# First steps of a staged Fourier transform, on quarters with sums and differences, in a fused GFNet mixing and SoLU kernel

## The chip, the cores and the metric

The kernel runs on one core of a Trainium2 chip. The metric is the device time of one execution in microseconds (us). Before the change four runs took 1708.62 to 1714.92 us, with a median of 1712.42 us.

## What is computed

The first half filters each of eight sequences of 3136 tokens with 256 channels in the frequency domain. The second half takes all 25088 filtered tokens through a two-layer block with a SoLU activation and a layer norm. Everything is float32 at the outputs.

```python
# x (8, 3136, 256), filt_r and filt_i (1569, 256)
X = np.fft.rfft(x, axis=1)
y = np.fft.irfft(X * (filt_r + 1j * filt_i), n=3136, axis=1)
t = y.reshape(8 * 3136, 256)
h = t @ w_in                                   # w_in (256, 1024)
e = np.exp(h - h.max(-1, keepdims=True))
solu = h * e / (e.sum(-1, keepdims=True) + 1e-9)
ln = (solu - solu.mean(-1, keepdims=True)) / np.sqrt(solu.var(-1, keepdims=True) + 1e-6) * g_ln
out = ln @ w_out                               # w_out (1024, 256)
```

## The kernel before

**The transform.** A length of 3136 is 49 times 64. Token number n1*64+n2 has n1 from 0 to 48 and n2 from 0 to 63. For each sequence ("entry", 0 to 7) three stages follow each other:

- *First steps* (`first`, L204; matmuls at L211, named pa). The 64 values of n2 are taken in 8 pieces. A piece has four values from the front and their four mirrored ones (63-n2) from the back. `fetch_x` (L194) loads it as a tile of 98 rows, 49 for each of the two halves, by 4x256. Two matmuls ("halves" u=0 and u=1) multiply it with the constant table wf (98x100), each over 512 columns (two values of n2 times 256 channels). Table rows of the mirrored half carry signs, so that sums and differences over the mirrored pair are taken inside the matmul. ScalarE (ACT) copies each result out of PSUM into a tile t1 (L213), and `store_first` (L215, L217) stores it to a scratch d1 in DRAM.
- *Spectrum* (`forward` L242, `multiply` L251, `inverse` L267). In 7 units, the second step on 64x64 blocks (matmuls at L239, named pb), the product with the filter (VectorE, L260 to L262; the last addition or subtraction of some units is on GpSimd), and the first step of the way back (again L239, named pc). The pb and pc matmuls have 64 rows and 64 columns of weights each and lie in the four quadrants of the array. The result is stored in a scratch d2.
- *Steps back* (`fetch_back` L285, `back` L294; matmuls at L300, named py). In 8 pieces of two groups each they write the filtered tokens, channels on partitions, into the resident tile y.

Entry 0 runs through all this ahead of the main loop. Entries 1 to 7 run inside it.

**The main loop.** `step(k)` (L837) is called for k from 0 to 204. A step handles one block of 128 tokens, and two steps, an even and an odd one, make a pair, in which both matrix products are done with seven instead of eight block products (sums of blocks come from GpSimd: `pair_sums` L607 and `project_sums` L713, both through L605). m (L627) are the matmuls of the first product, o (L739) those of the second. Between them: ACT keeps a half of h (L637), VectorE finishes h with its extremum (L648, L651), ACT takes the exponential (L659), VectorE normalizes (L675), ACT squares (L677), VectorE turns the block in 32x32 squares (L685), SyncE's queue regroups it by DMA to solu_t (L697), and the outputs are scaled (L751 to L758) and stored.

**The order of the work.** Nothing is scheduled by a tool: the instructions are issued in the order in which `step` calls them, and each engine goes through its own in that order. Per step there are lists of jobs: `stores[k]` at the start, `products[k]` in the middle of VectorE's work, `early[k]` and `mid[k]` between the matmuls, `late[k]` at the end, then `loads[k]`. The table PLAN gives, for each of entries 1 to 7, the steps of its 8 first pieces, 7 spectrum units and 8 pieces back. The half u=0 of a first piece stands in `early[t]`, u=1 in `late[t]`.

**Buffers and queues.** x tiles and the tiles t4 of the way back share a pool "r" of three buffers, t1 has a pool of three. Row loads are put into `loads` by a rule:

```python
row_loads.sort(key=lambda load: load[0])
for n, (t, earliest, load) in enumerate(row_loads):
    at = max(t - 3, earliest, min(row_loads[n - 3][0] + 1, t - 1) if n >= 3 else -1)
```

so a load stands at the end of step `at`, at most three steps ahead of its use t and not before the row tile three uses earlier is done. The x loads, the d1 and d2 stores, the t4 loads and the filter loads are issued on GpSimd's queue (POOL), between its sums. PSUM results pa, py and one of the m tiles take turns in two banks (`psum`, L515).

Of the kernel before, what the change touches and what calls it, by code (L numbers as in the profile page):

```python
# [17 lines left out]
P = 128  # L18
# [20 lines left out]
    ([0, 0, 0, 0, 1, 1, 1, 1], [4, 5, 6, 7, 8, 10, 12], [16, 17, 18, 19, 20, 20, 21, 22]),  # L39
    (range(3, 11), range(14, 28, 2), range(31, 47, 2)),  # L40
    ([11, 12, 13, 14, 15, 24, 26, 28], range(32, 46, 2), range(53, 69, 2)),
    (range(32, 48, 2), range(50, 64, 2), range(76, 92, 2)),
    (range(54, 70, 2), range(72, 86, 2), range(101, 117, 2)),
    (range(77, 93, 2), range(95, 109, 2), range(125, 141, 2)),
    (range(102, 118, 2), range(120, 134, 2), range(150, 166, 2)),
]
EPS_LN, EPS_SM = 1e-6, 1e-9


def dft_tables():  # L50


# [31 lines left out]
    f32 = np.float32  # L84
    return wf.reshape(NR, NK).astype(f32), wi.reshape(NK, NR).astype(f32), de.astype(f32)


@with_exitstack
def kernel(
# [9 lines left out]
):  # L99
    nc = tc.nc  # L100
    wf_host, wi_host, de_host = dft_tables()
    wf_dram = nc.inline_tensor(wf_host, name="wf_tbl").ap()
    wi_dram = nc.inline_tensor(wi_host, name="wi_tbl").ap()
    de_dram = nc.inline_tensor(de_host, name="de_tbl").ap()
# [13 lines left out]

    wf_t = consts.tile([NR, NK], FP32, name="wf_t")
    wi_t = consts.tile([NK, NR], FP32, name="wi_t")  # L120

# [47 lines left out]
    class Spectrum:  # L169
# [5 lines left out]
        def __init__(self, e, pools, load, load_de):  # L175
            self.e, self.pools = e, pools
            self.load, self.load_de = load, load_de
            self.spare = {}
            self.units = [(i, min(2, NP - i)) for i in range(0, NP, 2)]
            self.xs, self.t1s, self.t2s, self.fs, self.prods, self.gs, self.des, self.spectra = (  # L180
                {} for _ in range(8))

# [32 lines left out]
        def store_first(self, i, n0, store):  # L215
            t1 = self.t1s.pop((i, n0))
            store(d1[self.e].rearrange("s (a n) c -> (s a) n c", a=4)[  # L217
                :, NCH * i + n0:NCH * i + n0 + t1.shape[1], :], t1)

        def buffer(self, i, kind, shape):  # L220
# [86 lines left out]
    with ExitStack() as st:  # L307
# [158 lines left out]
        for i in range(units):  # L466
            if i + 2 < units:
                start(i + 2)
            sp.multiply(i, 0, nc.vector.tensor_tensor)
            sp.multiply(i, 1, nc.gpsimd.tensor_tensor)  # L470
            pss = [ps_t.tile([P, 2, C], FP32, name=f"pc_0_{i}_{u}", tag="t") for u in range(2)]
            idle(pss[0])
            sp.inverse(i, pss)
            sp.store(i, nc.scalar.dma_start)
            if i == 0:
                nc.gpsimd.dma_start(out=wi_t, in_=wi_dram)
                nc.gpsimd.dma_start(out=g_sb, in_=moe_g_ln.rearrange("(k p) -> p k", p=P))
            elif i in (1, 3, 4):
                begin({1: 2, 3: 3, 4: 4}[i])
# [38 lines left out]
    def psum_pair(name, other):  # L518
# [11 lines left out]
    pools |= {name: pool(name + "1", bufs)  # L530
             for name, bufs in (("r", 3), ("t1", 3), ("t2", 1), ("p", 1), ("g", 1))}
    pools["de"] = pool("de1", 2)
# [228 lines left out]
    def store_out(p):  # L761
# [10 lines left out]


    early, mid, late, stores, loads, products = (
        [[] for _ in range(blocks + LAG + 1)] for _ in range(6))
# [9 lines left out]
    for e in range(1, B):  # L785
# [5 lines left out]
        for i, t in enumerate(first_at):  # L791
            if i not in sp.xs:
                row_loads.append((t, -1, lambda sp=sp, i=i: sp.fetch_x(
                    i, [lambda out, in_: nc.gpsimd.dma_start(out=out, in_=in_)] * 2)))
            for u in range(2):
                (early, late)[u][t].append(lambda sp=sp, i=i, u=u: sp.first(
                    i, (u,), psum(f"pa_{sp.e}_{i}_{u}").rearrange("p a c -> p (a c)").rearrange(
                        "p (o n) -> p o n", o=1), nc.scalar.copy))
                ((early[t], late[t]) if t < 2 else (mid[t], stores[t + 1]))[u].append(
                    lambda sp=sp, i=i, u=u: sp.store_first(i, 2 * u, nc.gpsimd.dma_start))  # L800
        for i, t in enumerate(spectrum_at):
# [17 lines left out]
        for ch, t in enumerate(back_at):  # L819
            row_loads.append((t, spectrum_at[-1] + 2, lambda e=e, ch=ch: fetch_back(e, ch, pools["r"])))  # L820
            for cb in range(KD):
                (early, late)[cb][t].append(
                    lambda e=e, ch=ch, cb=cb: back(e, ch, cb, nc.scalar.copy))
    row_loads.sort(key=lambda load: load[0])
    for n, (t, earliest, load) in enumerate(row_loads):


        at = max(t - 3, earliest, min(row_loads[n - 3][0] + 1, t - 1) if n >= 3 else -1)
        assert at < t
# [7 lines left out]
    def step(k):  # L837
# [39 lines left out]
        if not odd:  # L877
# [6 lines left out]
            if 0 <= j - 3 < pairs:  # L884
                regroup(j - 3, 1)
            for job in mid[k]:
                job()
            if 0 <= j - 4 < pairs:
# [3 lines left out]
        else:  # L892
# [5 lines left out]
            if hid:  # L898
                product(j, 3)
                product(j, 4)  # L900
            for job in mid[k]:
                job()
            if 0 <= j - 3 < pairs:
# [13 lines left out]
        else:  # L917
# [3 lines left out]
            if proj:  # L921
                keep_out(p, 1, (1, 0))
        for job in late[k] + loads[k]:
            job()
# [37 lines left out]
```

## Time and profile before

| | us |
|---|---|
| median of four runs | 1712.42 |
| the profiled execution | 1714.54 |
| its span, first to last instruction | 1712.8 |
| PE (TensorE matmul) busy | 1634.7 |
| VectorE (DVE) busy | 1215.5 |
| GpSimd (POOL) busy | 1102.6 |
| ScalarE (ACT) busy | 945.5 |
| matmuls pa, from x (L211), 232 records | 127.5 |
| matmuls py (L300), 1024 records | 138.0 |
| ACT copies t<-pa (L213), 112 | 65.4 |
| DMA issues x<-in_x_dram on POOL (L794), 100, 683 ns each | 67.9 |
| DMA issues d<-t on POOL (L217), 112, 574 ns each | 64.3 |

A float32 matmul leaves two records on PE. Matmul records overlap, so that the distance between starts tells what one costs. Times inside the execution are counted from the span's start. The main loop begins at about 111 us; a step takes some 7 to 9 us, a pair of steps some 14 us where no transform work is in it and 18.2 us (817 to 853) where first steps, spectrum and steps back fall together. "A <- B" in a wait reads: A stood idle until B was done. The profile's mean TensorE clock is 0.976 of full speed; DMA moved 308.72 MB.

### The profile page before, as it was taken

How to read it: one execution, taken by the hardware profiler on the slowest of the kernel's cores; microseconds unless marked ns; L12 is line 12 of the kernel's file. 1: busy time of each engine (PE TensorE's matmuls, PEld its weight loads, DVE VectorE, ACT ScalarE, POOL GpSimd, SP SyncE). 2: the span in 40 equal slices, each digit the busy share in tenths (PEclk: the TensorE clock that was granted, in tenths of full speed). 3: DMA queues.
4: the chain of work that ended last, by engine and by line, in shares of the span. 5: the costliest groups of instructions: out<-in, count | busy, mean ns of one | idle time of the engine just before them, and what ended most of it. 6: DMA issues, size and time to landing. Idle time of an engine off the chain costs nothing.

```text
span 1712.8 us, 30324 instructions
## 1 busy us (share of the span) xinstructions
PE 1634.7 (95%) x9816; PEld 1122.1 (66%) x9816; DVE 1215.5 (71%) x2583; ACT 945.5 (55%) x1734; POOL 1102.6 (64%) x1319
## 2 busy tenths in 40 slices
PE   6778899899999999999999999999999999999996
PEld 2353366666666666766677666766777777777776
DVE  1675676577776787677766787678877777777772
ACT  2144556465656556656566455655556666656551
POOL 5354876455766767757666667666756766667663
PEclk8978899899999999999999999999999999999999
DMA  9885878667886787667865786657754454444443
GB/s 258 242 265 172 269 239 228 178 169 181 236 248 178 193 238 216 169 162 216 240 180 143 198 233 181 159 146 219 214 131 111 112 140 114 102 111 106 109 108 93
DMA packets 367329, 308.72 MB, mean 180 GB/s; under 512 B 63802, under 2 KB 333011, under 8 KB 367171
## 3 DMA queue, kind: packets, MB, share of 16 engines
q1 hardware_dynamic: 287684, 147.59, 33.9%
q0 software_dynamic: 42592, 120.91, 23.8%
q10 hardware_dynamic: 36896, 38.28, 7.7%
q8 instruction: 80, 1.31, 0.3%
q14 instruction: 77, 0.63, 0.1%
HBM read 121.82 MB, written 81.50 MB: 119 GB/s over the span
## 4 chain that ended last, share of the span: by engine, by line
PE 74%; DMA 10%; DVE 8%; POOL 3%; issue 2%; ACT 2%; SPq 1%; POOLq 0%; ACTq 0%; DVEq 0%
PE o L739 29%; PE m L627 29%; PE py L300 6%; PE pa L211 5%; DMA solu_t<-turn 4%; PE pb L239 3%; DVE h L675 2%; PE pc L239 2%; DMA x<-in_x_dram 1%; DMA t<-d 1%; SPq L697 1%; DMA out_dram<-ot 1%; POOL u L605 1%; ACT e L659 1%; DMA t<-x 1%
## 5 line engine op out<-in xcount | busy, mean ns | idle before, releaser
L677 ACT ACTIVATE e<-h,nmu 128x1024 f32<-128x1024 f32 x196 | 225.4, 1150 | 332.3 <-DVE h L675 328.9
L739 PE MATMUL o<-w_out_sb,solu_t 128*128 128x128 f32 x3136 | 402.7, 277 | 2.8 <-DVE ot L756 1.9
L739 PEld LDWEIGHTS o<-w_out_sb,solu_t 128*128 128x128 f32 x3136 | 380.7, 193 | 33.8 <-issue 28.6
L739 PEld LDWEIGHTS o<-w_out_sb,u 128*128 128x128 f32 x2352 | 306.5, 192 | 146.0 <-issue 113.9
L627 PE MATMUL m<-w_in_sb,s 128*128 128x512 f32 x784 | 399.1, 600 | 1.1 <-ACT h L637 1.1
L605 POOL TENSOR_TENSOR u<-solu_t 128x512 f32<-128x512 f32 x98 | 149.3, 1524 | 271.2 <-DMA solu_t<-turn 142.1
L739 PE MATMUL o<-w_out_sb,u 128*128 128x128 f32 x2352 | 311.9, 276 | 7.3 <-ACT ot L751 6.6
L627 PE MATMUL m<-w_in_sb,y 128*128 128x512 f32 x588 | 310.5, 612 | 6.3 <-DVE nmax L651 4.0
L675 DVE SCALAR_TENSOR_TENSOR h<-e,rsum,h 128x1024 f32<-128x1024 f32 x196 | 279.4, 1425 | 6.9
L758 DVE SCALAR_TENSOR_TENSOR ot<-o,rs_t,ot 128x128 f32<-128x128 f32 x294 | 102.7, 349 | 249.7 <-ACT ot L751 206.5
L685 DVE STREAM_TRANSPOSE turn<-h 128x1024 f32<-128x1024 f32 x196 | 242.7, 1238 | 1.7 <-DMA rows<-rs 0.4
L637 ACT COPY h<-m 128x512 f32<-128x512 f32 x294 | 172.5, 587 | 125.3 <-PE m L627 122.2
L659 ACT ACTIVATE e<-h,nmax 128x1024 f32<-128x1024 f32 x196 | 224.9, 1148 | 0.0
L651 DVE CUSTOM_DVE_ANT_0 h<-m,h 128x512 f32<-128x512 f32 x196 | 134.4, 686 | 113.2 <-ACT h L637 84.0
L605 POOL TENSOR_TENSOR u<-solu_t,u 128x512 f32<-128x512 f32 x98 | 138.2, 1410 | 100.6 <-PE o L739 96.7
L627 PEld LDWEIGHTS m<-w_in_sb,s 128*128 128x128 f32 x784 | 131.2, 192 | 86.5 <-issue 78.6
L300 PEld LDWEIGHTS py<-wi_t,t 100*128 100x128 f32 x1024 | 135.9, 200 | 51.2 <-issue 41.9
L627 PEld LDWEIGHTS m<-w_in_sb,y 128*128 128x128 f32 x588 | 100.0, 195 | 81.6 <-issue 51.9
L605 POOL TENSOR_TENSOR solu_t<-solu_t,solu_t 128x512 f32<-128x512 f32 x98 | 146.5, 1495 | 7.7
L300 PE MATMUL py<-wi_t,t 100*128 100x98 f32 x1024 | 138.0, 282 | 13.1 <-DMA t<-d 8.9
L303 ACT COPY y<-py 128x392 f32<-128x392 f32 x128 | 108.1, 846 | 69.8 <-PE py L300 67.0
L211 PE MATMUL pa<-x,wf_t 98*100 98x512 f32 x232 | 127.5, 643 | 11.9 <-DMA x<-in_x_dram 10.1
(96 smaller groups left out, 1931.9 us busy)
## 6 DMA issues: line engine op xcount, KB each, us to landing
solu_t<-turn SPq DMA_DIRECT2D x784, 128.0 KB
out_dram<-ot SPq DMA_DIRECT2D x196, 128.0 KB
d<-t POOLq DMA_DIRECT2D x112, 200.0 KB, 4.7
t<-d POOLq DMA_DIRECT2D x56, 400.0 KB, 5.3
x<-in_x_dram POOLq DMA_DIRECT2D x108, 196.0 KB, 5.7
f<-f_dram POOLq DMA_DIRECT2D x39, 512.0 KB, 7.1
d<-g POOLq DMA_DIRECT2D x39, 512.0 KB, 6.1
t<-d ACTq DMA_DIRECT2D x36, 512.0 KB
```

Of the source, the lines that this page charges most:

```text
L211: nc.tensor.matmul(out=ps[0:NK, j], lhsT=wf_t, rhs=self.xs[i][0:NR, 2 * u:2 * u + 2, :], start=True, stop=True)
L300: nc.tensor.matmul(out=psv[:, i:2 * NCH - i:2 * NCH - 1 - 2 * i, :], lhsT=t4s[e, ch][:, i, cb * P:cb * P + P], rhs=wi_t, start=True, stop= ...
L303: evac(out=y[:, cb, t0:t0 + S].rearrange("p (r m j) -> p m j r", m=N2 // NCH, j=NCH)[:, ch:last + 1 - ch:last - 2 * ch], in_=psv.rearrange ...
L605: nc.gpsimd.tensor_tensor(out=out, in0=in0, in1=in1, op=op)
L627: nc.tensor.matmul(out=ms[j, bank], lhsT=lhsT, rhs=w_in_sb[:, w, :], start=m in (1, 2, 7), stop=True, skip_group_check=True)
L637: nc.scalar.copy(out=h_half(k, i), in_=ms[j, 0])
L651: nc.vector.tensor_tensor_reduce(out=h_half(k, i), in0=ms[j, bank], in1=h_half(*kept), scale=1.0, scalar=sofar, op0=ALU.add, op1=ALU.min, ...
L659: nc.scalar.activation(out=e, in_=hs[k], func=AFT.Exp, bias=nmaxs.pop(k)[:, 1:2], scale=-1.0, accum_out=esum)
L675: nc.vector.scalar_tensor_tensor(out=solu, in0=e, scalar=rsum, in1=solu, op0=ALU.mult, op1=ALU.mult, accum_out=nmu)
L677: nc.scalar.activation(out=e, in_=solu, func=AFT.Square, bias=nmu, scale=-float(DFF), accum_out=variances[g][:, i:i + 1])
L685: nc.vector.transpose(out=turns[g][:, :, i, :], in_=solus.pop(k).rearrange("p (f j) -> p f j", j=32))
L739: nc.tensor.matmul(out=pos[p, bank], lhsT=lhs[:, f, :], rhs=w[:, f, :], start=f == 0 and m in (1, 2, 7), stop=True, skip_group_check=True)
```

## The change

It touches the first steps of entries 1 to 7, the table PLAN and the rule for row loads.

- Entries 2 to 7: a piece is loaded by `fetch_quarters` with its rows 0 to 48 holding two of the four values n2 and rows 64 to 112 the other two, and with the mirrored values in the columns beside them, so that sum and difference over the mirrored pair can be taken elementwise. Four loads take the place of two; for the first group 64 rows are read instead of 49, save in entry 7. `difference` (VectorE) writes a new tile, for which there is one buffer; `sum` (GpSimd) is done in place.
- `first_quarters` multiplies with a new table wq (128x2x64): four matmuls over 512 columns, 49 rows each, with 64 columns of weights for the sums and 50 for the differences, one in each quadrant of the array. ACT makes two copies of 114 rows by 512 back into the x tile, and `store_quarters` stores it with two DMAs of 50 rows by 4 KB.
- In a piece's step t, which is odd: the loads stand at the end of step t-3, or up to t-2 where a buffer is not free sooner; the difference stands in `products[t-1]` and the sum at the end of step t-1, ahead of that step's loads; the matmuls stand at the end of step t (or in the early place for the first of two pieces with the same t); the stores stand at the start of step t+1.
- Entry 1 keeps its matmuls, but copies results back into its x tile and stores right after each.
- Pool "r" has four buffers instead of three and the rule looks four uses back; pool t1 is gone. wq is loaded once on GpSimd's queue before the main loop.
- Steps back stand in even steps, spectrum units start in even steps too.

```diff
 PLAN = [
     None,
     ([0, 0, 0, 0, 1, 1, 1, 1], [4, 5, 6, 7, 8, 10, 12], [16, 17, 18, 19, 20, 20, 21, 22]),
-    (range(3, 11), range(14, 28, 2), range(31, 47, 2)),
-    ([11, 12, 13, 14, 15, 24, 26, 28], range(32, 46, 2), range(53, 69, 2)),
-    (range(32, 48, 2), range(50, 64, 2), range(76, 92, 2)),
-    (range(54, 70, 2), range(72, 86, 2), range(101, 117, 2)),
-    (range(77, 93, 2), range(95, 109, 2), range(125, 141, 2)),
-    (range(102, 118, 2), range(120, 134, 2), range(150, 166, 2)),
+    ([3, 5, 7, 9, 9, 11, 11, 13], range(16, 30, 2), range(32, 48, 2)),
+    ([15, 23, 25, 27, 29, 31, 33, 35], range(38, 52, 2), range(54, 70, 2)),
+    (range(39, 55, 2), range(58, 72, 2), range(76, 92, 2)),
+    (range(63, 79, 2), range(82, 96, 2), range(100, 116, 2)),
+    (range(87, 103, 2), range(106, 120, 2), range(126, 142, 2)),
+    (range(111, 127, 2), range(130, 144, 2), range(150, 166, 2)),
 ]
...
+        def fetch_quarters(self, i, dma):
+            self.xs[i] = out = self.pools["r"].tile([P, NCH, C], FP32, name=f"x_{self.e}_{i}", tag="r")
+            xb = x[self.e]
+            for g in range(2):
+                for h, first, step in ((0, NCH * i + 2 * g, C), (1, N2 - 1 - NCH * i - 2 * g, -C)):
+                    parts = [(64, N1)] if g else [(0, 64)] if self.e + 1 < B else [(0, N1), (N1, 64 - N1)]
+                    for p, n in parts:
+                        dma(out=out[p:p + n, 2 * h:2 * h + 2, :],
+                            in_=bass.AP(tensor=xb.tensor, offset=xb.offset + first * C,
+                                        ap=[[N2 * C, n], [step, 2], [1, C]]))
+        def difference(self, i):
+            rows = slice(0, 64 + N1)
+            xi = self.xs[i]
+            self.diffs[i] = diff = self.pools["diff"].tile([P, 2, C], FP32, name=f"diff_{self.e}_{i}",
+                                                           tag="diff")
+            nc.vector.tensor_tensor(out=diff[rows], in0=xi[rows, 2:4, :], in1=xi[rows, 0:2, :],
+                                    op=ALU.subtract)
+        def sum(self, i):
+            rows = slice(0, 64 + N1)
+            xi = self.xs[i]
+            nc.gpsimd.tensor_tensor(out=xi[rows, 0:2, :], in0=xi[rows, 0:2, :], in1=xi[rows, 2:4, :],
+                                    op=ALU.add)
+        def first_quarters(self, i, pss):
+            xi, diff = self.xs[i], self.diffs.pop(i)
+            for j, rhs in enumerate((xi[:, 0:2, :], diff)):
+                for g in range(2):
+                    rows = (64, NK // 2)[j]
+                    nc.tensor.matmul(out=pss[g][64 * j:64 * j + rows],
+                                     lhsT=wq_t[64 * g:64 * g + N1, j, 0:rows],
+                                     rhs=rhs[64 * g:64 * g + N1], start=True, stop=True)
+            rows = slice(0, 64 + NK // 2)
+            for g in range(2):
+                nc.scalar.copy(out=xi[rows, 2 * g:2 * g + 2, :], in_=pss[g][rows])
+        def store_quarters(self, i, dma):
+            xi = self.xs.pop(i)
+            rows = d1[self.e].rearrange("s (b j n) c -> j (s b) n c", b=2, j=2)
+            for j in range(2):
+                dma(out=rows[j, :, NCH * i:NCH * i + NCH, :], in_=xi[64 * j:64 * j + NK // 2])
...
-             for name, bufs in (("r", 3), ("t1", 3), ("t2", 1), ("p", 1), ("g", 1))}
+             for name, bufs in (("r", 4), ("diff", 1), ("t2", 1), ("p", 1), ("g", 1))}
...
+            dma = nc.gpsimd.dma_start
+            if e == 1:
+                for u in range(2):
+                    (early, late)[u][t].append(lambda sp=sp, i=i, u=u: sp.first(
+                        i, (u,), psum(f"pa_{sp.e}_{i}_{u}").rearrange("p a c -> p (a c)").rearrange(
+                            "p (o n) -> p o n", o=1), nc.scalar.copy, sp.xs[i][0:NK, 2 * u:2 * u + 2, :]))
+                    (early, late)[u][t].append(lambda sp=sp, i=i, u=u: sp.store_first(
+                        i, 2 * u, nc.gpsimd.dma_start))
+            else:
+                row_loads.append((t, t - 2, -1, lambda sp=sp, i=i, dma=dma: sp.fetch_quarters(i, dma)))
+                products[t - 1].append(lambda sp=sp, i=i: sp.difference(i))
+                sums_after[t - 1].append(lambda sp=sp, i=i: sp.sum(i))
+                first_of_two = t in first_at[i + 1:]
+                (early if first_of_two else late)[t].append(lambda sp=sp, i=i: sp.first_quarters(
+                    i, [psum(f"pa_{sp.e}_{i}_{g}") for g in range(2)]))
+                stores[t + 1].append(lambda sp=sp, i=i, dma=dma: sp.store_quarters(i, dma))
...
-        at = max(t - 3, earliest, min(row_loads[n - 3][0] + 1, t - 1) if n >= 3 else -1)
+        at = max(t - 3, earliest, min(row_loads[n - 4][0] + 1, latest) if n >= 4 else -1)
...
-        for job in late[k] + loads[k]:
+        for job in late[k] + sums_after[k] + loads[k]:
```

## The prediction

> **What bounds the kernel now.** First the page's busy times and its chain, to see which engine sets the end; then the timeline of TensorE in a settled pair of steps; then where TensorE stood still.
>
> ```profile
> span 1712.8 us, 30324 instructions
> ...
> PE 1634.7 (95%) x9816; PEld 1122.1 (66%) x9816; DVE 1215.5 (71%) x2583; ACT 945.5 (55%) x1734; POOL 1102.6 (64%) x1319
> ...
> PE 74%; DMA 10%; DVE 8%; POOL 3%; issue 2%; ACT 2%; SPq 1%; POOLq 0%; ACTq 0%; DVEq 0%
> ```
>
> PE is busy for 95%, and three quarters of the chain is PE. By stretches of 100 us it is 98 to 100 busy in nearly all from 400 to 1600 us: there, matmul time taken away is time gained until something else is late. The timeline shows what the first steps cost and what four-quadrant matmuls cost (columns: start, length, line, output<-inputs; starts are what count, the ends overlap).
>
> ```profile
> 822.32 0.44 PE L239 MATMUL pc<-pr,de 64*64 64x256 f32 x2
> ...
> 823.36 1.10 PE L211 MATMUL pa<-x,wf_t 98*100 98x512 f32 x2
> 824.30 1.02 PE L627 MATMUL m<-w_in_sb,y 128*128 128x512 f32 x2
> ...
> 826.91 1.03 PE L300 MATMUL py<-wi_t,t 100*128 100x98 f32 x8
> 827.88 1.11 PE L239 MATMUL pb<-t,de 64*64 64x256 f32 x16
> 828.92 1.12 PE L627 MATMUL m<-w_in_sb,s 128*128 128x512 f32 x2
> 829.88 1.05 PE L739 MATMUL o<-w_out_sb,u 128*128 128x128 f32 x8
> ...
> 834.28 1.02 PE L211 MATMUL pa<-x,wf_t 98*100 98x512 f32 x2
> 835.14 1.95 PE L739 MATMUL o<-w_out_sb,solu_t 128*128 128x128 f32 x16
> ```
>
> One first-step matmul of 512 columns holds PE for 0.86 us (834.28 to 835.14), or 0.94 behind another form (823.36 to 824.30); a piece has two. The eight 64x64x256 matmuls of pb, two in each quadrant, take 1.04 us together (827.88 to 828.92), those of pc as well (822.32 to 823.36). 256 columns should take half of 0.86, so eight one after another would be 3.4 us: the quadrants overlap.
>
> PE's stalls, with what ended them, from its timeline early in the run:
>
> ```profile
> 118.46 3.19 PE L211 MATMUL pa<-y,wf_t 98*100 98x512 f32 x4 [1.47 <-ACT t L213]
> ...
> 128.09 4.53 PE L211 MATMUL pa<-y,wf_t 98*100 98x512 f32 x6 [3.40 <-ACT t L213]
> ...
> 177.35 1.98 PE L239 MATMUL pc<-pi,de 64*64 64x256 f32 x8 [2.65 <-POOL pi L262]
> ...
> 199.62 1.09 PE L239 MATMUL pc<-pi,de 64*64 64x256 f32 x8 [3.56 <-POOL pi L262]
> ...
> 317.92 2.00 PE L300 MATMUL py<-wi_t,t 100*128 100x98 f32 x8 [3.08 <-DMA t<-d]
> ...
> 334.46 2.00 PE L300 MATMUL py<-wi_t,t 100*128 100x98 f32 x8 [5.26 <-DMA t<-d]
> ```
>
> Read the length beside the wait: the same py takes 0.87 us at 826.91 and about 1.9 here. After a stall PE runs some 4 us at half speed, so a stall costs more than its wait.
>
> **What the Trainium skill says.** "TensorEngine Tiling (Array Packing)", Tiling Modes: four 64x64 tiles run independently, and a change of mode drains TensorE. The trace agrees: 1.04 us for pb, and about 0.1 us on either side (py before pb holds 0.97 instead of 0.87, m after it 0.96 instead of 0.86). "TensorE: Matmul & The Clock Gate", Part 1: the clock halves after an idle window and is given back after some microseconds of work; the doubled lengths above agree. "SBUF — State Buffer" (its rule on the shared port pair): a VectorE tensor_tensor with both inputs in SBUF and a GpSimd operation exclude each other; this fits L262 on DVE, 0.69 us at 837.34 but 854 ns on average, and POOL's 1.27 against a mean of 1.4 to 1.5.
>
> **The change, part by part.** Base: the profiled execution, 1714.5 us with a span of 1712.8; the median of the four runs, 1712.4, is 2 below, and I take that off at the end.
>
> (A) *The matmuls.* Before, from step 9 on, 42 pieces are left (two of entry 2, eight each of 3 to 7), each 0.86+0.90 = 1.76 us: 73.9. After, 45 are left in that stretch, since entries 2 and 3 are spread out. A piece is four matmuls of 512 columns, one in each quadrant, the columns per quadrant of a pb. No row of before shows this form with 49 rows and 50 or 64 columns: lower bound 0.86 (all four together), upper 1.72 (two by two); I take pb's 1.04. Behind a pc (29 pieces) the mode is already set; 16 pieces pay 2x0.1 for it. 45x1.04+16x0.2 = 50.0. Gain 24 us (32 at the lower bound; a loss of 7 at the upper).
>
> (B) *The stall of the steps back.* The py at 317.92 and 334.46 belong to steps 20 and 21 of entry 1's way back. By the rule at L828 with three row buffers their loads stood at the end of steps 19 and 20; with four buffers they come at 18 and 19, one step (8 us) sooner. The waits were 3.1 and 5.3; the half-speed records behind them cost about 3 more each (py +1.1, pb +0.9, m +1.0; then py +0.9, o +1.7, m +0.6). All gone: 14 us. Lower bound 0, if POOL issues them late.
>
> (C) *Entry 1's first steps* no longer copy into t1 but back into their own x tile, so the copy does not wait for a store to land (ACT t<-pa waited 6.9 us for d<-t at 127.46). PE's four waits sum to 5.9 us, with half speed 8. The next step's preparation of w_out on DVE (L578, 4.1 us) stays, so no more than that.
>
> (D) *POOL at steps 4 to 7.* There pi is added on POOL (L262) and PE waits for it. Ahead of it in POOL's queue now come a sum (x tile, 113x512, priced as L605's 128x512: 1.4) and four x loads at 0.68 instead of two; one store (0.57) moves out of the way, and DVE's difference (0.7 to 0.85, as L262) shifts pi's inputs. Step 5: 1.4+1.35-0.57+0.85 = 3.0 later. Ahead of step 7 stand the loads of both pieces of step 9, eight instead of two: 1.4+4.0-0.57+0.85 = 5.7. PE's own work there shrinks but it only waits longer. Sum +9. Bounds 0 and +12.
>
> (E) *One difference buffer.* Steps 9 and 11 take two pieces each, and both differences stand in the step before. The second must wait until PE has read the first, at the start of step 9 or 11. Behind it on DVE are queued the normalization (1.5), a multiply (2.1), a turn (1.24) and the finish (0.7) that frees a bank of m: with the difference 6.4 us after the quarters, where PE reaches that bank after 2.7 (16 o and one m). Stall 3.7, and a little more in step 11, which has output work too: with slower records +10 for both. Bounds +3 and +14.
>
> (F) *Step 23's piece.* Its buffer comes free only for a load at the end of step 21, so its difference, some 3.5 us into step 22, waits for it. POOL ends its sums 2 to 4 us into the next step (u and solu_t at 844.04 to 846.6, where PE's step begins at 842.5), four issues 2.7, landing 5.3 (median of x between 400 and 1200 us): landed at 10 to 12. DVE stands 6 to 8 us; its slack (below) takes some: +7. Bounds 0 and +9.
>
> (G) *All other pieces*, 40 of them: sum and difference run beside PE. DVE has room: in an even step
>
> ```profile
> 830.98 0.35 DVE L756 TENSOR_SCALAR ot<-o,rs_t 128x128 f32<-128x128 f32 x1 [1.51 <-PE o L739]
> 831.87 0.35 DVE L758 SCALAR_TENSOR_TENSOR ot<-o,rs_t,ot 128x128 f32<-128x128 f32 x1 [0.54 <-PE o L739]
> ```
>
> DVE waits 2.05 us for PE; 0.85 fits. POOL per pair of steps gets one sum (1.4) and two issues more (1.4) and has 4 to 6 us of waiting for solu_t (5.56 at 825.28). The load three steps ahead: POOL's last sum of an even step ends about 7.8 us into it (it waits for PE's o), then the sum 1.4, f 0.7, four issues 2.7: 12.6, landing 5.3 later at 18; the difference stands at 17.5+3.5 = 21. Three us in hand. Copies keep their number (two of 512 columns), stores too (twice 200 KB). ACT's copy frees the bank that m takes 1.75 us later; it needs 0.6 plus a start of 0.3. Cost +1 for a late load here and there. If the cover goes: rival 2.
>
> Sum: -24-14-8+9+10+7+1 = -19: 1695.5 profiled, 1693 as a median.
>
> **Rivals.** (1) *The start's queues give way*: D, E and F cost 4 together, since POOL and DVE get to their work sooner than I count; 1693-22 = 1671, taking 1660 to 1680. For it: POOL waits 6 us on ACT at 155 to 167; against: the chain passes through POOL at both pi. (2) *Loads late in every pair*, the slower side: the difference waits on DVE for x, everything behind it too. DVE's spare 1.2 us in the even step and 1.7 before the finish in the odd one (835.44 ends 836.1, PE needs it at 837.8) make, with the 3 us in hand, 6 us: from a landing above 11.2 us on, each us more costs 1 us in 40 pieces. At 12.2: 1693+40 = 1733; it decides the sign from about 11.7. Landings of x between 400 and 1200 us are 3.3 to 9.4, so this is against the profile. (3) *The quadrants don't overlap four ways*, so that the change does not do what it says: A is a loss of 7 instead of a gain of 24: 1724. Against: pb, pc. (4) *B stays*, POOL being too late for the t loads still: 1707.
>
> **How the numbers follow.** Forecast 0.56 (own range 1680 to 1705), rival 1 0.20, rival 2 0.08, rival 3 0.04, rival 4 0.12. Faster by over 0.3% (below 1707.3; a measurement of this kernel tells about 0.3% from no change): the first two and half of the fourth, 0.81. Within 0.3%: 0.07. Slower: 0.12. The range 1666 to 1711 leaves out rivals 2 and 3 and the low end of 1.
>
> **What would show it.** In the profile after: four pa records starting nearly together, 0.9 to 1.1 us to the next form; no t<-d wait of PE at steps 20 and 21; no pa wait for ACT at 118 to 142; pi waits of 5 to 9 us at steps 5 and 7; DVE waiting for PE ahead of a diff twice, and once for x, with an m or o wait on PE behind; POOL near 1240 busy, DVE near 1255. I am wrong if PE is below 93% busy between 400 and 1200, or if pa holds PE for 1.7 us.

## The result and the profile after

| | us |
|---|---|
| before, median of 56 runs | 1714.97 |
| after, median of 35 runs | 1709.78 |
| ratio after to before | 0.997 [0.996, 0.998] |
| forecast | 1693 |

The change gains 5 us; the prediction had 19, from the 1712.4 that four runs gave then down to 1693. In this section, "before" and "after" are the profiled executions. The one of after took 1719.97 us, some 10 above its own median, so waits read from it can be too large, and what a part costs in the whole time is taken from medians and ratios further below.

The busy times and the chain of after:

```profile
span 1718.2 us, 31117 instructions
...
PE 1609.7 (94%) x10008; PEld 1108.7 (65%) x10008; DVE 1271.3 (74%) x2631; ACT 938.5 (55%) x1734; POOL 1264.8 (74%) x1480
...
PE 66%; DMA 14%; DVE 7%; POOL 6%; issue 4%; ACT 2%; SPq 1%; ACTq 0%; DVEq 0%; POOLq 0%
```

PE is 25 us less busy, and the span is not shorter. The chain says where it went: PE has 66% of it instead of 74, DMA and POOL have more. VectorE has 56 us more work, GpSimd 162.

One piece of quarters on TensorE, from the timeline of after (start, length, line, output<-inputs):

```profile
224.07 0.60 PE L260 MATMUL pa<-x,wq_t 49*64 49x512 f32 x2
224.10 0.60 PE L260 MATMUL pa<-diff,wq_t 49*50 49x512 f32 x2
224.51 0.60 PE L260 MATMUL pa<-x,wq_t 49*64 49x512 f32 x2
224.53 0.60 PE L260 MATMUL pa<-diff,wq_t 49*50 49x512 f32 x2
225.06 1.13 PE L681 MATMUL m<-w_in_sb,y 128*128 128x512 f32 x2
```

The first of the four starts at 224.07, the next form at 225.06: a piece holds PE for 0.99 us. The price taken for part A was 1.04. Now the places that answer to the stalls of before:

```profile
167.31 0.70 PE L292 MATMUL pc<-pi,de 64*64 64x256 f32 x2 [5.41 <-POOL pi L315]
...
194.21 0.70 PE L292 MATMUL pc<-pi,de 64*64 64x256 f32 x2 [9.07 <-POOL pi L315]
...
239.03 3.78 PE L793 MATMUL o<-w_out_sb,solu_t 128*128 128x128 f32 x16 [3.53 <-DVE ot L810]
...
282.78 1.10 PE L353 MATMUL py<-wi_t,t 100*128 100x98 f32 x8 [1.16 <-DMA t<-d]
```

The waits for pi are the two of before, at least twice as long: 5.41 and 9.07 instead of 2.65 and 3.56 (D). At 239, where two pieces share a step, a new one: an output's bank that VectorE has not freed (E). Of the steps back, only one t<-d wait is left, at another place, 1.16 us; those of 3.08 and 5.26 at steps 20 and 21 are gone (B). The four waits of pa for ACT's t, 5.9 us in before, are gone too (C).

TensorE's waits between 400 and 1600 us in after (line, releaser: us in total, times, longest), then the two of them that are listed for before, and the group of the difference on VectorE over the whole run:

```profile
PE o L793 <- DVE ot L810: 8.7, 7, 2.8
PE m L681 <- DVE nmax L705: 6.5, 8, 1.2
PE o L793 <- DVE rsum L724: 3.2, 10, 1.1
```

```profile
PE m L627 <- DVE nmax L651: 1.2, 2, 0.7
...
PE o L739 <- DVE rsum L670: 0.9, 5, 0.2
```

```profile
L245 DVE TENSOR_TENSOR diff<-x x48: 681/693/2667, 138.3 to 1178.0; 113x512 f32<-113x512 f32 x48
its engine sat idle before it (us, times) until:
  DMA x<-in_x_dram: 26.6, 13
  PE pa L260: 12.5, 2
```

None of the three waits had over 1.2 us in before; all name VectorE. The kernel e1 below, which does the same from step 24 on, has 3.3, 5.3 and 2.8 us of them, 11 instead of 18, so part of their size belongs to this one execution. VectorE in turn stood still ahead of the difference for 26.6 us in 13 places because x had not landed; the first of these, 4.95 us at step 22, is F. One of the others, on VectorE, GpSimd and TensorE:

```profile
562.29 0.68 DVE L705 CUSTOM_DVE_ANT_0 h<-m,h 128x512 f32<-128x512 f32 x1
...
565.91 1.65 DVE L245 TENSOR_TENSOR diff<-x 113x512 f32<-113x512 f32 x1 [2.93 <-DMA x<-in_x_dram]
...
567.85 1.90 DVE L729 SCALAR_TENSOR_TENSOR h<-e,rsum,h 128x1024 f32<-128x1024 f32 x1
```

```profile
557.76 0.77 POOL L236 DMA_DIRECT2D x<-in_x_dram  x1
...
567.07 1.60 POOL L659 TENSOR_TENSOR u<-solu_t,u 128x512 f32<-128x512 f32 x1
568.63 2.25 POOL L251 TENSOR_TENSOR x<-x 113x512 f32<-113x512 f32 x1
```

```profile
570.08 2.05 PE L793 MATMUL o<-w_out_sb,solu_t 128*128 128x128 f32 x16 [2.43 <-DVE ot L810]
...
574.24 1.12 PE L681 MATMUL m<-w_in_sb,y 128*128 128x512 f32 x2 [1.25 <-DVE nmax L705]
```

Read it from the top. VectorE ends L705 at 562.98 and takes up the difference next, since its queue is in order. The last of the four x loads was issued at 557.76; the difference starts when it has landed, 8.15 us later, at 565.91. The difference then takes 1.65 us instead of 0.69, its median, and the normalization L729 behind it 1.90, with GpSimd's two-operand instructions beside them. The two ot and the normalization come that much later, and TensorE waits 2.43 us for ot and 1.25 for nmax.

### The profile page after: what moved, and what is told of

It reads as the page before. It is cut to its first block, busy times and chain, and to the rows that moved or that the text cites. A ratio compares the mean times of both kernels' runs of the same rounds, so it can differ in the third digit from the quotient of the medians.

```text
span 1718.2 us, 31117 instructions
## 1 busy us (share of the span) xinstructions
PE 1609.7 (94%) x10008; PEld 1108.7 (65%) x10008; DVE 1271.3 (74%) x2631; ACT 938.5 (55%) x1734; POOL 1264.8 (74%) x1480
## 4 chain that ended last, share of the span: by engine, by line
PE 66%; DMA 14%; DVE 7%; POOL 6%; issue 4%; ACT 2%; SPq 1%; ACTq 0%; DVEq 0%; POOLq 0%
PE o L793 27%; PE m L681 25%; PE py L353 5%; DMA solu_t<-turn 4%; DMA x<-in_x_dram 3%; DVE h L729 3%; PE pc L292 2%; DMA de<-de_tbl 2%; PE pa L260 2%; PE pb L292 2%; POOL x L236 1%; PE pa L217 1%; DMA y<-in_x_dram 1%; DVE diff L245 1%; POOL u L659 1%
## 5 line engine op out<-in xcount | busy, mean ns | idle before, releaser
L793 PEld LDWEIGHTS o<-w_out_sb,solu_t 128*128 128x128 f32 x3136 | 385.5, 195 | 77.1 <-issue 33.3
L793 PE MATMUL o<-w_out_sb,solu_t 128*128 128x128 f32 x3136 | 407.7, 279 | 25.2 <-DVE ot L810 16.3
L681 PE MATMUL m<-w_in_sb,s 128*128 128x512 f32 x784 | 405.8, 609 | 4.4 <-ACT h L691 4.2
L681 PE MATMUL m<-w_in_sb,y 128*128 128x512 f32 x588 | 315.6, 620 | 11.8 <-DVE nmax L705 9.6
L659 POOL TENSOR_TENSOR u<-solu_t 128x512 f32<-128x512 f32 x98 | 143.9, 1468 | 216.1 <-DMA solu_t<-turn 120.1
L729 DVE SCALAR_TENSOR_TENSOR h<-e,rsum,h 128x1024 f32<-128x1024 f32 x196 | 296.7, 1514 | 6.9
L659 POOL TENSOR_TENSOR u<-solu_t,u 128x512 f32<-128x512 f32 x98 | 149.3, 1523 | 75.3 <-PE o L793 70.7
L705 DVE CUSTOM_DVE_ANT_0 h<-m,h 128x512 f32<-128x512 f32 x196 | 133.9, 683 | 93.4 <-ACT h L691 59.9
L681 PEld LDWEIGHTS m<-w_in_sb,s 128*128 128x128 f32 x784 | 125.7, 192 | 64.9 <-issue 56.9
L659 POOL TENSOR_TENSOR u<-u,solu_t 128x512 f32<-128x512 f32 x98 | 138.3, 1411 | 0.7
```

The costliest lines, as they stand in the source:

```text
L659: nc.gpsimd.tensor_tensor(out=out, in0=in0, in1=in1, op=op)
L681: nc.tensor.matmul(out=ms[j, bank], lhsT=lhsT, rhs=w_in_sb[:, w, :], start=m in (1, 2, 7), stop=True, skip_group_check=True)
L705: nc.vector.tensor_tensor_reduce(out=h_half(k, i), in0=ms[j, bank], in1=h_half(*kept), scale=1.0, scalar=sofar, op0=ALU.add, op1=ALU.min, ...
L729: nc.vector.scalar_tensor_tensor(out=solu, in0=e, scalar=rsum, in1=solu, op0=ALU.mult, op1=ALU.mult, accum_out=nmu)
L793: nc.tensor.matmul(out=pos[p, bank], lhsT=lhs[:, f, :], rhs=w[:, f, :], start=f == 0 and m in (1, 2, 7), stop=True, skip_group_check=True)
```

## The experiments

The ladder of times, each as its ratio to the kernel before on the same chip, and that ratio times 1715 us. The time given with an experiment below is the median of its own runs, so it can differ from the last column by a few us.

| kernel | ratio, 95% interval | us |
|---|---|---|
| after | 0.997 [0.996, 0.998] | 1710 |
| e1 own buffer for the second difference | 0.9934 [0.9911, 0.9958] | 1704 |
| e2 e1, difference behind the normalization | 0.9911 [0.9883, 0.9939] | 1700 |
| e3 e1, all x loads on SyncE | 0.9912 [0.989, 0.9934] | 1700 |
| e4 after, no sum, no difference | 0.9752 [0.9725, 0.9778] | 1672 |
| e5 after, no sum | 0.9897 [0.984, 0.9953] | 1697 |
| e6 after, no difference | 0.9786 [0.975, 0.9822] | 1678 |
| e7 before, buffers of after | 0.9888 [0.9859, 0.9918] | 1696 |
| e8 e2, entry 2's x on SyncE | 0.987 [0.9833, 0.9906] | 1693 |
| e9 after, difference of ready data | 0.9862 [0.9834, 0.989] | 1691 |
| e10 e8, difference on GpSimd | 0.9953 [0.9909, 0.9996] | 1707 |
| e11 e8, every other difference on GpSimd | 0.989 [0.9854, 0.9926] | 1696 |
| e12 e8, last piece's sum and difference a step later | 1.0144 [1.01, 1.0188] | 1740 |
| e13 e8, no sum, no difference | 0.9744 [0.9698, 0.9791] | 1671 |
| e14 e8, entry 2 on halves | 0.9823 [0.9798, 0.9848] | 1685 |

A step between two rows carries both intervals, some 4 to 7 us; where less than that is read below, it is from the profiled executions, by comparing the starts of ACT's copy h<-m pair by pair. "Pair 6-7" is the pair of steps 6 and 7.

**e1: the second difference of a step gets a place of its own** (part E alone undone).

```diff
+            if out is None:
+                out = self.pools["diff"].tile([P, 2, C], FP32, name=f"diff_{self.e}_{i}", tag="diff")
...
+                second_of_two = spare[1][:, 10 * C:12 * C].rearrange("p (n c) -> p n c", c=C) if t in first_at[:i] else None
+                products[t - 1].append(lambda sp=sp, i=i, out=second_of_two: sp.difference(i, out))
```

> The changed kernel with a place of its own for the difference of the second piece of steps 9 and 11 (an idle stretch of y), so that it need not wait until PE has read the first. Theory A (term E, mis-sized: one difference buffer holds DVE, behind it ACT and PE): the pairs of steps 8-9 and 10-11 fall from 26.3 and 24.2 us to about 19 and 18, together 13 to 14, so about 1697 against the changed kernel's 1709.8. Rival B (these pairs are held by POOL's queue with its eight x loads, and the wait for the buffer only hides that): both pairs stay above 23 us and the time stays within 4 us of 1709.8.

1704.03 us, between the theories: pair 8-9 fell from 26.31 to 21.32 us, pair 10-11 only from 24.18 to 23.19. So E is real and costs 6 us, not 10. What stays too long in these pairs is in part GpSimd's: TensorE waits there for the sum, 6.3 us in two places, where after has 2.4. The difference still waited for x, 23.4 us in 14 places.

**e2: the difference behind the normalization and the outputs in VectorE's queue** (on top of e1).

```diff
-                products[t - 1].append(lambda sp=sp, i=i, out=second_of_two: sp.difference(i, out))
+                differences[t - 1].append(lambda sp=sp, i=i, out=second_of_two: sp.difference(i, out))
...
-        for job in late[k] + sums_after[k] + loads[k]:
+        for job in differences[k] + late[k] + sums_after[k] + loads[k]:
```

> As e1, and the difference stands after the normalization and the output scaling of its step instead of ahead of them. Theory A (from step 24 on, what the quarters save on PE is lost because the difference waits for x at the head of DVE's queue, with the normalization, the outputs and the finish behind it): another 8 to 15 us below e1, and PE's waits for DVE (o for ot, m for nmax) between 400 and 1200 us fall from about 20 to under 8 us. Rival B (DVE is simply full in the pairs with spectrum work, by the difference itself and by its lock against POOL's sums): within 4 us of e1.

1701.34 us. From e2's views of the difference and of TensorE's waits, 400 to 1340 us:

```profile
L246 DVE TENSOR_TENSOR diff<-x x46: 674/814/1769, 143.9 to 1163.8; 113x512 f32<-113x512 f32 x46
...
  POOL x L252: 16.6, 19
```

```profile
PE m L682 <- DVE nmax L706: 5.8, 12, 0.8
PE o L794 <- DVE rsum L725: 2.8, 13, 0.4
```

VectorE no longer waits for x and TensorE no longer for ot, but now GpSimd's sum waits for the difference (16.6 us, 19 times), and nmax is late as before. The wait was passed on rather than removed; the step from e1, some 3 us, is within the intervals.

**e3: the x loads of entries 2 to 7 on SyncE's queue** (on top of e1).

```diff
-                row_loads.append((t, t - 2, -1, lambda sp=sp, i=i, dma=dma: sp.fetch_quarters(i, dma)))
+                row_loads.append((t, t - 2, -1, lambda sp=sp, i=i: sp.fetch_quarters(i, nc.sync.dma_start)))
```

> As e1, and the x loads of entries 2 to 7 are issued on SyncE's queue instead of POOL's. Theory A (x lands late because POOL comes to its issue late): the difference's waits for x (26.6 us in 13 waits) go under 8 us, the two waits of pc for pi at steps 5 and 7 (5.4 and 9.1 us) fall to 3 to 5, POOL is busy 110 to 130 us less, and the time is 12 to 20 us below e1. Rival B (x lands late because the DMA engines are loaded, or the regrouping of solu_t that uses the same queue is held up): the waits move to solu_t and the time is that of e1 or above it.

1700.83 us, some 4 us below e1 and not 12 to 20. The waits for pi fell to

```profile
PE pc L293 <- POOL pi L316: 7.0, 2, 3.6
```

from 14.5 in after, and pair 6-7 from 26.90 to 20.31: part D was the x loads that GpSimd issues ahead of pi. It stood 20.3 us ahead of before at step 24 and 15.5 at step 150: later in the run x was late more often on SyncE's queue (the difference waited 32.8 us, 21 times).

**e4: neither sums nor differences.**

```diff
-            for j, rhs in enumerate((xi[:, 0:2, :], diff)):
+            for j, rhs in enumerate((xi[:, 0:2, :], xi[:, 2:4, :])):
...
-                products[t - 1].append(lambda sp=sp, i=i: sp.difference(i))
-                sums_after[t - 1].append(lambda sp=sp, i=i: sp.sum(i))
```

> The changed kernel without the sums and differences: the four matmuls of a piece take the two halves of the x tile as they were loaded, so that part of the computation is left out. Matmuls, loads, stores and plan are the same. Theory A (the elementwise work, its waits and its locks eat the gain): without it the start loses its stall (15 us), the pi waits shrink by some 3 to 5, and from step 24 on PE saves what was predicted, 20 to 27 us more than now: 1660 to 1672. Rival B (the quarters' loads, stores, the new plan or the matmuls themselves eat it): only the start's stall goes, 1690 to 1697.

1673.32 us. The 96 elementwise instructions, whose busy time lies beside TensorE's, cost 37 us together. The waits for pi stay (13.6 us, pair 6-7 26.78): they are the loads, as e3 says.

**e5 and e6: one of the two left out.** e5 drops the second of e4's removed lines, e6 the first and the operand.

> The kernel after, without GpSimd's sum (the second factor's first operand is the raw upper half, so the output is not the reference's); the difference on VectorE, all loads and all quarters stay. Theory 1 (GpSimd's time and the shared SBUF port: the sum delays x, pi and stretches VectorE's h and difference): 1690 us or less, h back at about 1430 ns mean from 1514, and the pairs from step 24 on cheaper by about 0.2 us each. Theory 2 (what costs is VectorE: the difference that stands ahead of its queue and waits for x): within 10 us of the kernel after, 1700 or more.

> The kernel after, without VectorE's difference (the raw mirrored half takes its place as the operand, so the output is not the reference's); GpSimd's sum and everything else stay. Theory 2 (VectorE's head-of-queue work and its wait for x): about 1682 us, with TensorE's waits for nmax, rsum and ot gone from the stretch 400 to 1600 us, and pairs 8-9 and 10-11 back under 20 us. Theory 1 (the sum): about 1700, no better than e5.

1701.28 and 1680.57 us. VectorE's difference carries most of the cost: 25 us (e5 to e4) to 32 (after to e6) of the 37; the sum carries 6 (e6 to e4) to 12 (after to e5). Without the sum, h took 1499 ns on average against 1514 in after and 1425 in before, so the sum's hold on the shared port is not the main thing; without the difference, h took 1440 and of TensorE's three waits shown above only rsum's, 1.0 us, is still listed.

**e7: the kernel before with the buffers of after** (B and C alone).

```diff
-             for name, bufs in (("r", 3), ("t1", 3), ("t2", 1), ("p", 1), ("g", 1))}
+             for name, bufs in (("r", 4), ("t2", 1), ("p", 1), ("g", 1))}
...
-                        "p (o n) -> p o n", o=1), nc.scalar.copy))
+                        "p (o n) -> p o n", o=1), nc.scalar.copy, sp.xs[i][0:NK, 2 * u:2 * u + 2, :]))
...
-        at = max(t - 3, earliest, min(row_loads[n - 3][0] + 1, t - 1) if n >= 3 else -1)
+        at = max(t - 3, earliest, min(row_loads[n - 4][0] + 1, t - 1) if n >= 4 else -1)
```

> The kernel before, with only what the change does to the buffers: the spectral step's copy goes in place for every entry, the separate pool is dropped, r has four buffers, so entry 1's start and the steps back at 20 and 21 have no wait; first steps stay on two halves, without sums, differences or quarters, in their old places. If the parts B and C of the prediction (-14 and -8) stand by themselves: about 1692 us. If in-place copies make the loads of x wait for stores instead: 1705 or more.

1696.03 us. Pair 0-1 went from 35.57 to 25.82 us, pair 20-21 from 34.72 to 20.22; from then on nearly every pair takes what it took before, within 1.5 us. So three lines of bookkeeping gain 19 us, and everything else in the change loses 14.

**e8: e2 with entry 2's loads alone on SyncE.**

```diff
-                row_loads.append((t, t - 2, -1, lambda sp=sp, i=i, dma=dma: sp.fetch_quarters(i, dma)))
+                row_loads.append((t, t - 2, -1, lambda sp=sp, i=i, dma=nc.sync.dma_start if e == 2 else dma: sp.fetch_quarters(i, dma)))
```

> e2 (second buffer for the difference, difference behind the normalization) with the x loads of entry 2 alone on SyncE's queue. If the waits for pi in steps 4 to 7 come from the x loads that GpSimd issues ahead of pi: pairs 4-5 and 6-7 fall from 20.3 and 26.9 us to about 19 and 20, and the time to 1693 us, with the rest as in e2. If the time of these waits is given back later: about 1700, as e2.

1695.13 us. Pairs 4-5 and 6-7 took 17.35 and 21.00 us (e2: 20.53 and 28.00), so part D is undone. Of these 10 us some 6 are left at step 24 (13.4 us ahead of before, e2 7.8): pair 16-17 took 25.34 us instead of 19.53, and in it TensorE waits 3.73 us ahead of a step back, for t<-d.

**e9: the same difference, of data that lies ready.**

```diff
-            nc.vector.tensor_tensor(out=diff[rows], in0=xi[rows, 2:4, :], in1=xi[rows, 0:2, :],
+            nc.vector.tensor_tensor(out=diff[rows], in0=w_in_sb[rows, 0, :].rearrange("p (n c) -> p n c", c=C),
+                                    in1=w_in_sb[rows, 1, :].rearrange("p (n c) -> p n c", c=C),
```

> The kernel after, with the difference formed on VectorE in the same place, of the same size and into the same buffer, but of two weight tiles that lie ready instead of x (so the output is not the reference's): VectorE's work stays, its wait for x is gone. The step between the kernel after (1709.8) and the one without a difference (1680.6) is about 29 us. Theory W (the wait for x at the head of VectorE's queue): 1692 or less, and TensorE's waits for ot, nmax and rsum from 400 to 1340 us fall from about 18 us to under 6. Theory T (VectorE's own time for it, 48 times 0.7 to 2.7 us): 1700 or more, waits as before.

1693.88 us, and of the three waits of TensorE for VectorE, 400 to 1340 us, are left

```profile
PE o L794 <- DVE ot L811: 1.5, 4, 0.6
PE o L794 <- DVE rsum L725: 1.2, 4, 0.4
...
PE m L682 <- DVE nmax L706: 0.7, 1, 0.7
```

VectorE's work is all there (48 times, median 690 ns), but x is not waited for: 16 to 18 us of the some 30 that the difference costs (medians and ratios) hang on this wait. Pair 22, where F was, took 17.87 us (22.36 in after), so 4.5 of the gain are F. Another wait goes with it: the sum overwrites what the difference reads, and GpSimd stood idle until the difference was done in four places of after, 8.3 us, all of them up to step 22, and in none of e9. Up to 3 us of the gain can be this (steps 8 to 11 took 47.6 us, 50.5 in after). The one buffer (12.5 us of waiting for pa, two times) is in e9 still, so another 6 are E, and the rest, some 7 by subtraction, would be the work itself.

**e10 and e11: the difference, or every other one, on GpSimd.**

```diff
-            nc.vector.tensor_tensor(out=diff[rows], in0=xi[rows, 2:4, :], in1=xi[rows, 0:2, :],
+            nc.gpsimd.tensor_tensor(out=diff[rows], in0=xi[rows, 2:4, :], in1=xi[rows, 0:2, :],
...
-                differences[t - 1].append(lambda sp=sp, i=i, out=second_of_two: sp.difference(i, out))
+                sums_after[t - 1].append(lambda sp=sp, i=i, out=second_of_two: sp.difference(i, out))
```

(In e11, only where i is odd.)

> e8 (second buffer, entry 2's x on SyncE's queue) with the difference moved from VectorE to GpSimd, ahead of the sum there. Theory T (in e8 it is VectorE's time that is left to gain): near the runs without a difference, 1680 to 1686 us. Rival (GpSimd has 70% busy and issues loads; 46 more operations of about 1.4 us delay x, pi and s, and lock VectorE's h): 1698 or more, with TensorE waiting for pi or s.

> e8 with the difference of every other piece on GpSimd, so that in a pair with two pieces each engine has one. If both engines are near their limits in such pairs: better than both e8 (1695) and e10, about 1687. If one engine alone is the limit: between e8 and e10.

1705.91 and 1696.05 us. On GpSimd a difference takes 1276 ns at the median, and the pair's sum behind it becomes late: TensorE waits for it 9.8 us between 400 and 1340 us, where e2 has 0.4. Half and half is no better than e8. The theory that VectorE's time is all that is missing falls; what is moved to GpSimd is late there.

**e12: sum and difference of a pair's last piece in the odd step, behind its finish.**

```diff
-                differences[t - 1].append(lambda sp=sp, i=i, out=second_of_two: sp.difference(i, out))
-                sums_after[t - 1].append(lambda sp=sp, i=i: sp.sum(i))
...
+                (differences[t - 1] if first_of_two else products[t]).append(
+                    lambda sp=sp, i=i, out=second_of_two: sp.difference(i, out))
+                (sums_after[t - 1] if first_of_two else products[t]).append(lambda sp=sp, i=i: sp.sum(i))
```

> e8 (second buffer, difference behind the normalization, entry 2's x on SyncE's queue), with the difference and the sum of the last piece of a pair not at the end of the even step, but in the odd one, behind its finish, where its x has landed by then. If what e8 still loses against the runs without a difference is VectorE's work crowded at the end of the even step: 1684 to 1690 us, TensorE's waits for nmax from 400 to 1340 us down from 7.3 us to under 3. If VectorE and GpSimd are short of time in both steps alike, or the sum beside the odd step's h locks the port: 1695 or more.

1735.61 us, slower than before; the second theory had 1695 or more, but nothing of this size. Its longest waits, 400 to 1340 us:

```profile
PE pa L261 <- POOL x L252: 31.6, 22, 2.3
PE o L794 <- DVE rsum L725: 9.2, 15, 1.3
```

nmax is off the list of long waits, as hoped, but the quarters now wait for GpSimd's sum in 22 places: it stands there behind the token sums s of the next pair (in one step s ends at 964.65 and the sum at 965.87, where TensorE waited 1.39 us). So of the places tried for the two operations (after, e2, e12) the end of the even step stays the best. Loads issued a step sooner, which would give them more room, were not tried.

**e13: e8 without sums and differences**, by e4's edit.

> e8 without sums and differences (raw halves as operands, so the output is not the reference's): the quarters' matmuls and the places and buffers of the change, with the issue of entry 2's loads off GpSimd. Beside e7 (1696; the buffers without quarters) it measures part A of the prediction (-24) by itself. If A is right: about 1672, and pairs 6-7 near 21 us. If A gives less than half of what was counted: 1684 or more.

1670.00 us, 26 below e7; by the ratios 0.9744 against 0.9888, 25 us. Its PE is busy for

```profile
PE 1591.8 (95%) x10008; PEld 1102.4 (66%) x10008; DVE 1219.0 (73%) x2583; ACT 941.1 (56%) x1734; POOL 1157.3 (69%) x1400
```

against 1624.0 in e7. Part A is there at full size when its operands cost nothing; e13 and e7 differ in the places of PLAN and in the loads too, so the 25 us are net of these.

**e14: e8 with entry 2's first steps on two halves as before.**

```diff
-            if e == 1:
+            if e <= 2:
...
-                row_loads.append((t, t - 2, -1, lambda sp=sp, i=i, dma=nc.sync.dma_start if e == 2 else dma: sp.fetch_quarters(i, dma)))
+                row_loads.append((t, t - 2, -1, lambda sp=sp, i=i, dma=dma: sp.fetch_quarters(i, dma)))
```

> e8 with entry 2's first steps as they were, on two halves, two matmuls a piece, no sums, no differences, each half copied in place, its x loads on GpSimd's queue two a piece; entries 3 to 7 keep the quarters. e8 stands at -1 us at step 18 against the kernel before, e7 (no quarters) at -10, the quarters without elementwise work at -19; after step 24 e8 loses no more on balance. If the rest of the loss sits in entry 2's crowded steps: -24 us at step 24 as in e7, 1687 to 1692 us in all. If entries 3 to 7 lose as much behind that: 1696 or more, no better than e7.

1684.41 us, 0.9823 [0.9798, 0.9848]: faster than before by 30 us, than after by 25 and than e7 by 11. At step 24 it stands 27.4 us ahead of before (e8: 13.4), at step 150 27.1 (e8: 16.4). The quarters of entries 3 to 7, with their new places and loads, are worth 11 us net (e7 to e14; the intervals leave 2 to 20); entry 2's eight pieces, in the crowded start, cost more than their matmuls save.

## Why the prediction was wrong

The mechanisms were right in six parts of seven, the sum was not: the failing step is (G), "All other pieces".

- (A), -24: right. A piece holds PE 0.99 us (1.04 taken); e13 against e7 is -25 by the ratios. Rival 3 falls.
- (B), -14, and (C), -8: right, -14.5 and about -10 in pairs 20-21 and 0-1; e7 gives -19 for both by its ratio.
- (D), +9: right in place; the size in part by luck. The pi waits grew by 8.3 us (14.5 against 6.2). The text gave the sum and the difference half of that (1.4 and 0.85 at each of the two), but without both (e4) the waits are still 13.6 us: the loads are the cause, as e3 and e8 show, and cost more than the time of their issue.
- (E), +10: right mechanism; 6 us by e1, within the bounds of 3 and 14.
- (F), +7: right mechanism. VectorE stood 4.95 us for x, and pair 22 took 22.36 us against 17.89 in e4, where no difference waits: 4.5.
- (G), +1: wrong. From e13 to after, 1671 to 1710, there are 39 us; D is 7 of them (e8 to e2), E 6, F 4.5. That leaves some 21 us, where the text had 1.

What of G failed, as it was put: "Three us in hand" between x's landing and the difference. By the starts in the profile of after, over the 32 pieces of entries 4 to 7, the last load of a piece had landed 0.4 us before VectorE came to the difference at the median (0.5 in e1); three pieces had 3 us or more, and in 11 VectorE waited. In these 11 the last load was issued 13.8 us after the first copy h<-m of step t-3 and took 7.7 us to land, in the other 21 it was issued after 10.9 and took 5.9 (medians). So two things took the room. In the late places GpSimd came to the loads later. And the landing was taken from before's loads, two of 196 KB a piece, at 5.3 us; the new ones, four a piece on the same queue, take 6.5 at the median in the same stretch of 400 to 1200 us.

VectorE's queue then stood for x in 12 places, 21.7 us, besides F's. e9 takes these waits out and gains 16 to 18 us, 4.5 of them F's and up to 3 the sum's in the start, which leaves some 9 to 14 of the 21 to G's wait. So rival 2 was the mechanism, "the difference waits on DVE for x, everything behind it too", in 12 places instead of 40. It was given 0.08 because it was to cost only from a landing above 11.2 us on; no load in that stretch took more than 9.1, and it came all the same, since the room was not there. How the rest of the 21 divides, no run shows. The second half of the term is "DVE waits 2.05 us for PE; 0.85 fits": the step chosen for that was one without another crowding, and the instruction took 1024 ns on average, up to 2667. And the sum was to cost TensorE nothing, but in e1 steps 9 and 11 wait 6.3 us for it.

Also wrong in the outlook: PE was to fall below 93% busy between 400 and 1200 us if the forecast failed. It was 97% (778.0 of 800, against 792.9 before): the mark of 93% stood at 56 us of idle time, and the forecast failed with 22.

Open: how the 22 us by which e8 stays behind e13 divide between VectorE's time, GpSimd's time and the order of the two. e10, e11 and e12 each move one of them and none gains. Nor was the new PLAN run with the old matmuls, so what the places alone cost or gain is not shown. e14 says where, not which: it is 8 us better than e8 by the ratios and gives up 8 x 0.77 = 6 us of matmul time, so that some 14 of the 22 would belong to entry 2's steps 3 to 17. The starts point the same way: of 26 us between the profiled runs of e8 and e13, 19 stand at step 24.

## What to carry to other kernels

Moving work from the bounding engine to engines with a quarter of their time free is not free: the new instruction sits in an in-order queue, and what matters is whether its operand has landed when its turn comes, every time and not at the median. Price such an instruction with its wait and with the delay of what is queued behind it, not by its length alone, then look for a place in which its operand is ready and its result not yet due; here none of the three places tried was wide enough. And split a change on the chip: its quiet part (a fourth buffer, a copy in place) was worth 19 us, its loud part cost 14 until it was left out where the queues are full.

## What the runs showed of the hardware

- Four float32 matmuls of 512 columns, 49 rows by 64 or 50 columns of weights, one in each quadrant, take 0.99 to 1.01 us together where nothing else stalls or slows TensorE: about what one takes on the full array (0.86) plus a change of form.
- A two-input tensor_tensor of 113x512 takes 0.69 us on VectorE at the median, and up to 2.67 us with two of GpSimd's beside it (790.49 in after); on GpSimd 1.27, and 2.25 beside VectorE's normalization (568.63). This fits the rule on the shared port pair that the prediction cites from the Trainium skill ("SBUF — State Buffer"), for instructions that both read from SBUF. The added sum has little part in the slowing of h: 1514 ns on average with it, 1499 without it (e5), 1440 without the difference (e6).
- What a stall does to the matmuls behind it cannot be told from its length alone. 16 o matmuls took 2.05 us behind a wait of 2.43 us, 3.78 behind one of 3.53 (1.95 without a wait, in before). But of the prediction's lines on pi, 8 pc took 1.98 us behind 2.65 and 1.09 behind 3.56; there the next pa, at 200.64, was the first slow one, with 1.75 us instead of 1.10.
- Four DMA issues in GpSimd's queue take 2.4 us (571.38 to 573.80). Put ahead of an instruction that TensorE waits for, the eight for step 9 delayed it by 5 us (pi at step 7: 9.07 in after, 3.7 in e8, which issues entry 2's loads on SyncE).
